# Attention with beacon keys, then a bilinear feed-forward net: the w1 and w2 products as seven block products, and a new order of all steps

## The chip, the cores and the metric

The kernel runs on one core of a Trainium2 chip. The metric is the device time of one execution in microseconds (us). A core has a matrix engine (PE; PEld is its weight load), VectorE (DVE), ScalarE (ACT), GpSimd (POOL) and SyncE (SP); the last two issue the transfers here. Matrix products go to PSUM, which holds 8 banks of 128 x 512 fp32 values; everything else is kept in SBUF.

## The reference, cut to what matters

```python
# q, k, v: (8, 8, 576, 64) fp32; beacon_k, beacon_v: (8, 8, 16, 64)
k_all = concatenate([beacon_k, k], axis=2)        # 592 keys
v_all = concatenate([beacon_v, v], axis=2)
scores = (1 / sqrt(64)) * matmul(q, k_all.T)      # beacons seen by all, k causal
a = exp(scores - max); a /= a.sum(-1) + 1e-9
x = matmul(a, v_all)                              # -> (4608, 512), heads side by side
y = ((x @ w1) * (x @ w2)) @ w3 @ w_out            # w1, w2: 512 x 1024; w3: 1024 x 1024; w_out: 1024 x 512
```

## The kernel before

Everything is in fp16 on the way into PE and in fp32 in PSUM. w3 @ w_out is computed once in the kernel (Wt, 1024 x 512), so that each token needs the products with w1, w2 and Wt only. The 4608 tokens are taken in two ways: attention goes by batch (8 batches of 576 tokens), the feed-forward part by chunks of 512 tokens (9 chunks, mc).

The order of all instructions is written out in one string, ORDER, a list of about 1170 short steps; the last line of the kernel walks through it and calls the function of each step. Each engine executes its own instructions in that order, and waits where a step needs what another engine has not finished. A step's last numbers are mostly PSUM banks, A or D name ACT or DVE, and S or P the queue that issues a transfer (SP or POOL). The steps are:

- loads: lq, lk, lv, lkb, lvb (q, k, v and beacons of a batch; batch 0's q and k come in fp32 on SP's queue, all others on POOL's, where they are cast to fp16), l1, l2 (quarters of w1, w2), l3 (128 rows of w3), lo (a quarter of w_out).
- q and k with the head's 64 values on the partitions: cast, tq/tk and eq/ek (transposes on PE and copies out of PSUM) or Dq/Dk (transposes by DMA, on SP's queue); tn and en for batch 0's beacons, tn waits for lkb 0.
- attention, in 13 groups g of score blocks per batch, four pairs of heads t: s (scores on PE, into two banks), exp (ACT, into the ring of 8 tiles), m (DVE, causal mask), v (PE, with the values), n (DVE: the reciprocal of the sums, then the scaling, into x16).
- x with its 512 columns on the partitions: x and ex (PE and a copy) or TX (by DMA), into xT.
- Wt: t3 and e3 (w3 transposed), f (PE, products with w_out), ew (copy).
- feed-forward, for 128 of the 1024 columns at a time (kf, 8 of them): a and b (PE, four matmuls each of 128x512), ea (the first product goes to SBUF in fp32, on ACT or DVE), eb (DVE: times the second product, into gT), then o (PE, 8 matmuls of 128x512 with Wt), eo (copy, on ACT or DVE) and st (out).

The lines of most use below: 546 (a, b on PE), 567 (o), 459 (f), 451 (t3), 474 (s), 505 (v), 531 (x), 484 (exp), 293 and 295 (ea and eo, on ACT and on DVE), 561 (eb), 494 (m), 516 and 517 (n), 377 (cast), 370 (l3). The trace writes w for w1 and w2 in SBUF, wo for w_out, va for v, and one or pair for PSUM banks. w3's rows lie in half of xT until they are used, so L370 writes xT.

```python
w316 = xT[:, :, ds(M // 2, 2 * DF)].rearrange("p a (c r) -> p a c r", c=2)
...
for line in ORDER.split(";"):
    kind, *args = line.split()
    ops[kind](*(int(arg) if arg.isdigit() else arg for arg in args))
```

Of the kernel before, what the change touches and what calls it, by code (L numbers as in the profile page):

```python
# [8 lines left out]
FP32 = mybir.dt.float32  # L9
# [59 lines left out]
f 3 0 7; f 2 0 6; exp 0 2 4; m 0 0 0; s 0 3 0; lv 0 4; f 3 1 7; exp 0 3 0; f 0 0 5; f 0 1 5; l3 7;
t3 1 4; exp 0 1 2; m 0 1 0; f 2 1 6; e3 1 D 4; s 0 4 0; s 0 5 2; lv 0 3; m 0 0 1; exp 0 4 0;  # L70
f 3 2 7; f 1 0 4; f 0 2 5; exp 0 5 2; lv 0 0; f 1 1 4; f 1 2 4; m 0 1 1; t3 5 3; lvb 0; f 3 3 7;
f 1 3 4; ew 3 A 7; tk 0 2 2; ew 1 D 4; l3 6; f 0 3 5; ek 0 2 A 2; f 2 2 6; ew 0 D 5; e3 5 A 3;
f 2 3 6; s 0 6 0; s 0 7 4; l2 2; ew 2 D 6; exp 0 6 0; f 5 0 7; l1 3; f 5 1 7; f 5 2 7; exp 0 7 4;
m 0 2 0; l3 4; f 5 3 7; ew 5 A 7; t3 7 6; lk 1 4 P; e3 7 A 6; lq 1 1 P; lkb 1; v 0 2 0 5;
v 0 1 0 7; lq 1 3 P; n 0 2 0 5; v 0 0 1 6; n 0 1 0 7; v 0 0 0 5; lk 1 0 P; s 0 8 2; s 0 9 0;
n 0 0 1 6; exp 0 8 2; t3 6 7; n 0 0 0 5; l2 3; v 0 1 1 6; e3 6 D 7; exp 0 9 0; f 7 0 5; m 0 2 1;
s 0 10 2; s 0 11 0; lq 1 2 P; m 0 3 0; exp 0 10 2; f 6 0 7; n 0 1 1 6; f 7 1 5; l2 1; t3 4 4;
exp 0 11 0; s 0 12 2; e3 4 D 4; l1 2; v 0 2 1 6; exp 0 12 2; m 0 3 1; tk 1 4 4; l1 1; f 7 2 5;
ek 1 4 D 4; f 7 3 5; n 0 2 1 6; lk 1 1 P; f 6 1 7; ew 7 A 5; v 0 3 0 4; lvb 1; tk 1 0 6; n 0 3 0 4;
tq 1 1 5; lq 1 4 P; ek 1 0 A 6; v 0 3 1 3; eq 1 1 D 5; x 0 0 4; lq 1 0 P; tq 1 3 6; n 0 3 1 3;  # L80
ex 0 0 A 4; f 6 2 7; f 6 3 7; eq 1 3 A 6; lk 2 0 P; tq 1 2 5; ew 6 D 7; x 0 3 4; eq 1 2 A 5;
x 0 1 6; x 0 2 3; ex 0 3 D 4; x 0 4 7; ex 0 1 A 6; lk 1 2 P; f 4 0 5; ex 0 2 D 3; f 4 1 5;
ex 0 4 A 7; f 4 2 5; f 4 3 5; lk 1 3 P; a 0 1 6; ew 4 A 5; a 0 7 7; ea 0 1 A 6; lv 1 0; a 0 0 6;
ea 0 7 A 7; lk 2 2 P; tq 1 4 7; tk 1 1 5; ea 0 0 A 6; lq 2 2 P; eq 1 4 D 7; a 0 4 4; ek 1 1 D 5;
lq 2 1 P; tq 1 0 6; b 0 7 7; eq 1 0 A 6; lv 1 3; tk 1 2 6; eb 0 7 7; b 0 1 5; ek 1 2 A 6; lv 1 4;
tk 1 3 6; lv 1 2; eb 0 1 5; a 0 3 7; ek 1 3 A 6; lv 1 1; ea 0 4 D 4; s 1 0 0; s 1 1 2; s 1 2 4;
# [101 lines left out]
def kernel(  # L188
# [93 lines left out]
    def bank(n):  # L282
        return shape(n, "one")
# [378 lines left out]
```

## Time and profile before

| | |
|---|---|
| median of 3 runs | 302.18 us (301.17 to 303.72) |
| the profiled execution, first to last instruction | 302.5 us |
| PE busy | 285.2 us (94%), 2850 matmuls |
| DVE, ACT, POOL busy | 149.9, 164.0, 131.8 us |
| mean granted TensorE clock | 0.966 |
| read from HBM, written to it | 39.32 MB, 9.44 MB |

How to read it: the profiled execution's 302.5 us stands 0.3 us above the median of the timed runs, so sums against it can be held against the median as they are. Busy is the time in which an engine had at least one instruction under way, so groups of pipelined matmuls overlap a little at their ends. The clock is in shares of 2.4 GHz: 1.00 is 2.4 GHz, 0.50 is 1.2 GHz.

### The profile page before, as it was taken

How to read it: one execution, taken by the hardware profiler on the slowest of the kernel's cores; microseconds unless marked ns; L12 is line 12 of the kernel's file. 1: busy time of each engine (PE TensorE's matmuls, PEld its weight loads, DVE VectorE, ACT ScalarE, POOL GpSimd, SP SyncE). 2: the span in 40 equal slices, each digit the busy share in tenths (PEclk: the TensorE clock that was granted, in tenths of full speed). 3: DMA queues.
4: the chain of work that ended last, by engine and by line, in shares of the span. 5: the costliest groups of instructions: out<-in, count | busy, mean ns of one | idle time of the engine just before them, and what ended most of it. 6: DMA issues, size and time to landing. Idle time of an engine off the chain costs nothing.

```text
span 302.5 us, 6941 instructions
## 1 busy us (share of the span) xinstructions
PE 285.2 (94%) x2850; PEld 153.2 (51%) x2850; DVE 149.9 (50%) x334; ACT 164.0 (54%) x214; POOL 131.8 (44%) x182
## 2 busy tenths in 40 slices
PE   6269999999999999997999999999999999999994
PEld 2154566456556465553545645554555455444441
DVE  4242574477278656671726535665462684134400
ACT  2246776687485578553628653755365265334332
POOL 8176888884297386760764375251002002000000
PEclk9657999999999999997999999999999999999999
DMA  7999999999999999999999999799316003500033
GB/s 186 242 205 183 184 185 153 129 158 135 173 197 141 144 187 173 155 144 153 147 151 152 131 183 197 96 167 205 50 49 145 0 2 113 106 0 0 2 139 138
DMA packets 159262, 40.85 MB, mean 135 GB/s; under 512 B 148736, under 2 KB 155392, under 8 KB 159232
## 3 DMA queue, kind: packets, MB, share of 16 engines
q0 software_dynamic: 114144, 25.83, 94.7%
q1 hardware_dynamic: 45088, 14.59, 32.3%
q8 instruction: 22, 0.36, 0.5%
q14 instruction: 8, 0.07, 0.1%
HBM read 39.32 MB, written 9.44 MB: 161 GB/s over the span
## 4 chain that ended last, share of the span: by engine, by line
PE 90%; DMA 4%; ACT 1%; DVE 1%; issue 1%; POOL 1%; POOLq 0%; DVEq 0%; ACTq 0%
PE one L546 42%; PE one L567 21%; PE one L505 10%; PE pair L474 9%; PE one L459 5%; DMA xT<-in_moe_w_dram 4%; PE one L451 1%; PE one L531 1%; PE one L395 1%; PE one L389 1%; DVE x L517 0%; ACT ring L484 0%; ACT gT L289 0%; POOL va L323 0%; DVE ring L494 0%
## 5 line engine op out<-in xcount | busy, mean ns | idle before, releaser
L546 PE MATMUL one<-xT,w 128*128 128x512 f16 x576 | 133.3, 381 | 2.5 <-issue 2.5
L484 ACT ACTIVATE ring<-pair 128x1024 f16<-128x1024 f32 x104 | 99.1, 1029 | 12.9 <-PE pair L474 12.7
L546 PEld LDWEIGHTS <-w 128*128 128x128 f16 x576 | 53.7, 98 | 63.8 <-issue 6.6
L561 DVE TENSOR_TENSOR gT<-one,asb 128x512 f16<-128x512 f32 x72 | 49.1, 689 | 46.4 <-ACT asb L293 25.2
L293 ACT ACTIVATE asb<-one 128x512 f32<-128x512 f32 x55 | 32.9, 597 | 65.7 <-PE one L546 50.9
L567 PE MATMUL one<-Wt,gT 128*128 128x512 f16 x288 | 66.1, 379 | 0.0
L580 POOL DMA_DIRECT2D out_dram<-st x28 | 15.8, 566 | 86.2 <-DVE rd L516 39.3
L567 PEld LDWEIGHTS <-gT 128*128 128x128 f16 x288 | 26.8, 98 | 30.0 <-issue 0.6
L323 POOL DMA_DIRECT2D va<-in_v_dram x40 | 34.0, 868 | 15.6 <-PE pair L474 8.6
L505 PEld LDWEIGHTS <-ring 128*128 128x128 f16 x960 | 34.4, 97 | 9.9 <-issue 2.4
L505 PE MATMUL one<-va,ring 128*128 128x65 f16 x960 | 37.5, 193 | 0.5 <-ACT gT L289 0.4
L293 ACT ACTIVATE st<-one 128x512 f32<-128x512 f32 x26 | 15.5, 597 | 35.5 <-PE one L567 35.5
L323 POOL DMA_DIRECT2D k<-in_k_dram x35 | 30.2, 863 | 7.8 <-DMA va<-in_v_dram 3.3
L517 DVE TENSOR_TENSOR x<-one,rd 128x384 f16<-128x384 f32 (+1 forms) x64 | 31.4, 491 | 2.2
L474 PE MATMUL pair<-qT,kT 64*128 64x80 f16 (+4 forms) x736 | 31.5, 231 | 0.7 <-ACT qT L289 0.7
L315 POOL DMA_DIRECT2D q<-in_q_dram x35 | 30.4, 872 | 2.9 <-DMA va<-in_v_dram 1.8
L474 PEld LDWEIGHTS <-kT 64*128 64x128 f16 x736 | 20.7, 98 | 17.5 <-issue 15.1
L516 DVE RECIPROCAL rd<-one 128x6 f32<-128x6 f32 (+1 forms) x64 | 11.8, 184 | 29.9 <-PE one L505 25.8
L494 DVE TENSOR_TENSOR ring<-ring,MD 128x768 f16<-128x768 f16 x32 | 17.7, 552 | 11.5 <-ACT ring L484 11.4
L459 PE MATMUL one<-wo,gT 128*128 128x512 f16 x64 | 17.3, 406 | 0.0
L494 DVE TENSOR_TENSOR ring<-ring,MX 128x384 f16<-128x384 f16 x32 | 11.3, 353 | 10.8 <-ACT ring L484 10.5
L295 DVE TENSOR_SCALAR asb<-one 128x512 f32<-128x512 f32 x17 | 11.6, 688 | 3.1 <-PE one L546 3.0
(53 smaller groups left out, 113.0 us busy)
## 6 DMA issues: line engine op xcount, KB each, us to landing
out_dram<-st POOLq DMA_DIRECT2D x28, 256.0 KB, 4.4
q<-in_q_dram POOLq DMA_DIRECT2D x28, 128.0 KB, 6.5
va<-in_v_dram POOLq DMA_DIRECT2D x24, 128.0 KB, 7.7
k<-in_k_dram POOLq DMA_DIRECT2D x21, 128.0 KB, 6.5
xT<-in_moe_w_dram POOLq DMA_DIRECT2D x8, 256.0 KB, 8.6
w<-in_moe_w_dram POOLq DMA_DIRECT2D x8, 256.0 KB, 7.2
out_dram<-st SPq DMA_DIRECT2D x8, 256.0 KB, 2.0
st<-in_k_dram SPq DMA_DIRECT2D x4, 288.0 KB, 5.4
```

Source lines behind the costliest of these rows:

```text
L293: nc.scalar.activation(dst, src, AF.Copy, scale=by)
L315: nc.gpsimd.dma_start(dst[:rows, c], src[b, :, ds(c * P, rows), :].rearrange("h s d -> s h d"))
L323: nc.gpsimd.dma_start(dst[ds(p0, rows), c], src[b, :, ds(s0, rows), :].rearrange("h s d -> s h d"))
L459: nc.tensor.matmul(bank(n), wT(r)[:, rt, :], wo16[:, rt, :], start=(rt == 0), stop=(rt == NFT - 1),)
L474: nc.tensor.matmul(shape(n, "pair")[:, hh, ds(col, w)], kT[ds(hh * 64, 64), t, ts(jt, P)], qT[ds(hh * 64, 64), t, ds(q0, w)],)
L484: nc.scalar.activation(held(b, g)[:, :, 0:GW], shape(n, "pair"), AF.Exp, scale=scale)
L494: nc.vector.tensor_tensor(blk, blk, msk, ALU.mult)
L505: nc.tensor.matmul(pv[:, 2 * at + hh, 0 : D + 1], held(b, g)[:, hh, ds(col, P)], va[:, jt, 2 * t + hh, 0 : D + 1], start=(jt == 0), stop=( ...
L517: nc.vector.tensor_tensor(x16s[b % NB2][:, ds(2 * h, ni), ts(t, P)].rearrange("p i (h d) -> p i h d", h=2), pv[:, 0 : 2 * ni, 0:D].rearran ...
L546: nc.tensor.matmul(bank(n), w12[:, kt, ds(i * DF + kf * P, P)], xT[:, kt, ds(mc * 512, 512)], start=(kt == 0), stop=(kt == NKT - 1),)
L561: nc.vector.tensor_tensor(gTs[mc % 2][:, kf, :], bank(n), asb[slot["asb", (mc, kf)]], ALU.mult)
L567: nc.tensor.matmul(bank(n), gTs[mc % 2][:, kf, ts(mt, P)], Wt[:, kf, :], start=(kf == 0), stop=(kf == NFT - 1),)
```

## The change

The feed-forward part goes by batch now, with halves of 288 tokens. For batches 1 to 7 the two products with w1 and w2 are seen as one product of 2 x 2 blocks: the token halves against the two halves of the 512 inner columns (a11, a12, a21, a22 in xT), and those against w1 and w2 (b11, b21, b12, b22). Four outputs are needed, namely both halves of the tokens with w1 and with w2. Instead of eight block products seven are made (step p, two matmuls of 128x288 each), from four sums S of blocks of x (step S, DVE, per batch) and four sums of blocks of w1, w2 (step T, DVE, once; one overwrites the first half of w2). PSUM adds up what it can: the order of one kf is

- p 5 and p 1 into two banks; ce (ACT) copies P5 to SBUF (es); c1 (ACT) copies P1 over P5 in its bank;
- p 6 adds to that bank (U2), p 2 adds to P1's bank (the first output);
- u (DVE): us = U2 + P5; then p 7 adds to U2's bank; p 3 goes into a third bank, t1 (DVE): us = P3 + us (the second output);
- t2 (DVE): es = U2 + P7 + P5 (the fourth output); then p 4 adds to U2's bank (the third output);
- g1 and g2 (DVE): the two elementwise products, 128x288, into gT.

Batch 0 is done plainly, in halves (a, b with four matmuls of 128x288, ea, and g). The factor 256 that ea applied is given by the ones column of v instead (ONE = 1/16, so that x is 16 times as large). gT holds two batches; o (now in four steps of two matmuls) still takes 128 tokens at a time.

The order is another one altogether. SP's queue has batch 0's k and q by pairs of heads; POOL's begins with batch 0's beacons and v. Here are POOL's first transfers before; in_moe_w is w1, w2 or w3 (L370 is l3, w3), in_v is lv, wo is w_out.

```order
L370 DMA xT<-in_moe_w_dram 128x1024
L323 DMA va_66<-in_v_dram 128x8x64
L370 DMA xT<-in_moe_w_dram 128x1024 x2
L348 DMA b_96<-in_beacon_k_dram 16x8x64
L373 DMA wo_61<-in_moe_w_out_dram 128x2x512 x2
...
L370 DMA xT<-in_moe_w_dram 128x1024
L373 DMA wo_61<-in_moe_w_out_dram 128x2x512
```

And the same queue from its start now (L412 is lkb, L387 lv, L425 a quarter of w1 or w2, L379 lq of batch 1).

```order
L412 DMA b_103<-in_beacon_k_dram 16x8x64
L387 DMA va_70<-in_v_dram 128x8x64
...
L387 DMA va_70<-in_v_dram 112x8x64
L425 DMA w_62<-in_moe_w_dram 128x4x256
L387 DMA va_70<-in_v_dram 80x8x64
L387 DMA va_70<-in_v_dram 128x8x64 x2
L420 DMA va_70<-in_beacon_v_dram 16x8x64
L379 DMA q_1_67<-in_q_dram 64x8x64
L425 DMA w_62<-in_moe_w_dram 128x4x256
```

The loads of w3 and w_out, their transposes and products (t3, f) moved behind batch 0's attention and feed-forward products. On PE, the first steps before were the transposes of batch 0's k and q and of w3 in turn (o16k and xT), then scores.

```order
L389 MATMUL one_104<-ident,o16k_90 128x96 [waits Pool_49]
L451 MATMUL one_104<-ident,xT 128x128 [waits Activation_49]
L389 MATMUL one_182<-ident,o16q_88 128x96
L389 MATMUL one_105<-ident,o16k_90 128x96 [waits Activation_49]
L451 MATMUL one_104<-ident,xT 128x128 [waits Activation_49]
L389 MATMUL one_105<-ident,o16q_89 128x96 [waits Activation_49]
```

PE's first steps now: the beacons' transposes, k and q of the first pair of heads (held in gT at that time), scores.

```order
L489 LDWEIGHTS b_103 [waits DMASW0_49]
L489 MATMUL ps<-ident,b_103 128x16 [waits Pool_49]
L453 LDWEIGHTS gT [waits DVE_49]
L453 MATMUL ps<-ident,gT 128x96
L453 MATMUL ps<-ident,gT 128x96 [waits Activation_49]
L537 LDWEIGHTS kT_74 [waits Activation_49]
L537 MATMUL ps<-qT_72,kT_74 128x128 [waits DVE_49]
```

The scores follow the first pair's transposes directly, with no w3 between. The third place is DVE in the middle of the feed-forward part. Before, one product in eb's form (L561) per kf stands among the steps of the next attention:

```order
L516 RECIPROCAL rd<-one_104 128x4
L517 TENSOR_TENSOR x_0_73<-one_104,rd 128x2x128
L516 RECIPROCAL rd<-one_2484 128x6
L517 TENSOR_TENSOR x_0_73<-one_2484,rd 128x3x128
L561 TENSOR_TENSOR gT_76<-one_2483,asb_78 128x512
L561 TENSOR_TENSOR gT_76<-one_104,asb_79 128x512
L561 TENSOR_TENSOR gT_76<-one_105,asb_77 128x512
L494 TENSOR_TENSOR ring<-ring,MX 128x2x192
```

Now u, t1, t2, g1, g2 (L686, L689, L692, L695, L700) of two or three kf at a time stand in turn (batch 5):

```order
L686 TENSOR_TENSOR us_84<-ps,es_80 128x288
L579 RECIPROCAL rd<-ps 128x6
L580 TENSOR_TENSOR x_0_77<-ps,rd 128x3x128
L689 TENSOR_TENSOR us_84<-ps,us_84 128x288
L692 TENSOR_TENSOR es_80<-ps,es_80 128x288
L695 TENSOR_TENSOR gT<-ps,us_84 128x288
L686 TENSOR_TENSOR us_85<-ps,es_81 128x288
L700 TENSOR_TENSOR gT<-ps,es_80 128x288
```

For each kf there are now five instructions of 128x288 per batch, each of which waits for PE or for an earlier one of the five, where there was one eb of 128x512 per chunk (and an ea, on DVE in 17 of 72 cases). Step counts that changed, in the whole list, before (now): a and b 72 + 72 with 512 columns (16 + 16 with 288), p 0 (392), ea 72 (16), eb or g 72 (16 + 112), ce, c1, u, t1, t2 0 (56 each), S 0 (28), T 0 (16), tq and tk 9 + 9 (14 + 14), Dq and Dk 30 + 30 (25 + 25), x 15 (20), TX 25 (20). Scores, exp, m, v, n, t3, f and o have the same instructions as before.

```diff
 ORDER = """
-consts 0; lk 0 0 S; lk 0 3 S; l3 0; consts 1; spin 10 7; lq 0 1 S; lv 0 2; lk 0 1 S; lq 0 3 S;
...
+lk 0 0 S; consts 0; lq 0 0 S; lkb 0; lk 0 1 S; lv 0 1; consts 3; spin 8 7; lq 0 1 S; lk 0 2 S;
...
-    xT = const.tile([P, NKT, M], FP16, name="xT")
+    xTs = [const.tile([P, NKT, S], FP16, name=f"xT_{i}") for i in range(NB2)]
+    Ss = [const.tile([P, 4, 2, HT], FP16, name=f"S_{i}") for i in range(NB2)]
+    T124 = const.tile([P, 3, 2, DF], FP16, name="T124")
...
-    gTs = [const.tile([P, NFT, 512], FP16, name=f"gT_{i}") for i in range(2)]
-    asb = [const.tile([P, 512], FP32, name=f"asb_{i}") for i in range(NASB)]
+    gT = const.tile([P, NFT, NG2], FP16, name="gT")
+    es = [const.tile([P, HT], FP32, name=f"es_{i}") for i in range(NES)]
+    us = [const.tile([P, HT], FP32, name=f"us_{i}") for i in range(NUS)]
...
-    w316 = xT[:, :, ds(M // 2, 2 * DF)].rearrange("p a (c r) -> p a c r", c=2)
+    def w316(r):
+        return sts[r].bitcast(FP16)[:, 0:DF]
...
+    def S_(b, i):
+        sv = Ss[b % NB2]
+        (a11, a12), (a21, a22) = quad(b)
+        in0, in1, op = {
+            1: (a21, a22, ALU.add),
+            2: (sv[:, 0], a11, ALU.subtract),
+            3: (a11, a21, ALU.subtract),
+            4: (a12, sv[:, 1], ALU.subtract),
+        }[i]
+        nc.vector.tensor_tensor(sv[:, i - 1], in0, in1, op)
...
+    def p(b, kf, i, n):
+        (a11, a12), (a21, a22) = quad(b)
...
+        mov, sta = {
+            1: (a11, b11),
+            2: (a12, b21),
+            3: (sv[:, 3], b22),
+            4: (a22, t4),
+            5: (sv[:, 0], t1),
+            6: (sv[:, 1], t2),
+            7: (sv[:, 2], t3),
+        }[i]
+        for j in (0, 1):
+            nc.tensor.matmul(
+                half(n),
+                sta[:, j],
+                mov[:, j],
+                start=(j == 0 and i in (1, 3, 5)),
+                stop=(j == 1),
+                skip_group_check=True,
+            )
...
-    def ea(mc, kf, e, n):
-        scaled(e, asb[take("asb", (mc, kf), NASB)], bank(n), GS)
+    def ea(b, kf, h, e, n, i):
+        copy(e, es[i], half(n))
...
+    def ce(n, i):
+        nc.scalar.copy(es[i], half(n))
+
+    def c1(na, ne):
+        nc.scalar.copy(half(ne), half(na))
+
+    def u(n, i, j):
+        nc.vector.tensor_tensor(us[j], half(n), es[i], ALU.add)
+
+    def t1(n, j):
+        nc.vector.tensor_tensor(us[j], half(n), us[j], ALU.add)
+
+    def t2(n, i):
+        nc.vector.tensor_tensor(es[i], half(n), es[i], ALU.add)
+
+    def g1(b, kf, n, j, us=us):
+        nc.vector.tensor_tensor(
+            gT[:, kf, ds((2 * b) % 4 * HT, HT)], half(n), us[j], ALU.mult
+        )
```

## Rows read from the trace of the kernel before

**Rows 1.** The page: the span in 40 slices of 7.56 us, three of its lines.

```profile
PE   6269999999999999997999999999999999999994
PEclk9657999999999999997999999999999999999999
GB/s 186 242 205 183 184 185 153 129 158 135 173 197 141 144 187 173 155 144 153 147 151 152 131 183 197 96 167 205 50 49 145 0 2 113 106 0 0 2 139 138
```

**Rows 2.** Chain of work that ended last, first 52 us: start, duration, what.

```profile
3.28 12.01 DMA xT<-in_moe_w_dram
...
20.59 0.65 ACT qT L289
21.28 1.46 PE pair L474 x22
...
48.23 0.86 PE one L531 x16
...
50.82 1.29 PE one L546 x6
```

**Rows 3.** The same chain, its longest pieces over the whole span.

```profile
257.03 27.74 PE one L546 x128
284.77 13.83 PE one L567 x64
```

**Rows 4.** The same chain, its last piece.

```profile
298.62 0.60 ACT st L293
```

**Rows 5.** Stretches: length, then PE, PEld, DVE, ACT, POOL busy, clock, DMA share, GB/s.

```profile
10.00:15.00 5.00, 0.66 (x6) 0.45 (x6) 1.31 (x3) 0.64 (x1) 0.26 (x1) 0.50 1.24 238
15.00:20.00 5.00, 3.27 (x34) 2.85 (x35) 2.02 (x4) 1.65 (x3) 3.75 (x6) 0.50 1.21 203
...
25.00:30.00 5.00, 5.00 (x38) 2.32 (x35) 1.51 (x3) 3.58 (x4) 2.81 (x6) 0.87 1.92 176
```

**Rows 6.** DVE and POOL in order of time, start of the kernel.

```profile
4.27 0.66 DVE L377 CAST o16k<-st 96x768 f16<-96x768 f32 x1 [1.96 <-DMA st<-in_k_dram]
8.44 0.56 DVE L377 CAST o16q<-st 96x768 f16<-96x768 f32 x1 [1.58 <-DMA st<-in_q_dram]
...
2.34 0.95 POOL L323 DMA_DIRECT2D va<-in_v_dram  x1
14.74 0.57 POOL L370 DMA_DIRECT2D xT<-in_moe_w_dram  x1 [5.60 <-DMA va<-in_v_dram]
```

**Rows 7.** Groups by line and shape: count, busy us, mean ns of one, idle before.

```profile
L517 DVE TENSOR_TENSOR x<-one,rd 128x384 f16<-128x384 f32 x32 | 17.8, 558 | 1.1
L517 DVE TENSOR_TENSOR x<-one,rd 128x256 f16<-128x256 f32 x32 | 13.6, 425 | 1.1
L494 DVE TENSOR_TENSOR ring<-ring,MD 128x768 f16<-128x768 f16 x32 | 17.7, 552 | 11.5 <-ACT ring L484 11.4
L494 DVE TENSOR_TENSOR ring<-ring,MX 128x384 f16<-128x384 f16 x32 | 11.3, 353 | 10.8 <-ACT ring L484 10.5
L289 ACT COPY xT<-one 128x320 f16<-128x320 f16 x2 | 0.9, 432 | 0.0
L293 ACT ACTIVATE asb<-one 128x512 f32<-128x512 f32 x55 | 32.9, 597 | 65.7 <-PE one L546 50.9 <-DVE gT L561 11.8 <-DVE x L517 2.4
```

**Rows 8.** The page's costliest groups, the scores and the products with v.

```profile
L505 PE MATMUL one<-va,ring 128*128 128x65 f16 x960 | 37.5, 193 | 0.5 <-ACT gT L289 0.4
L474 PE MATMUL pair<-qT,kT 64*128 64x80 f16 (+4 forms) x736 | 31.5, 231 | 0.7 <-ACT qT L289 0.7
```

**Rows 9.** DVE and ACT in order of time, 175 to 200 us.

```profile
184.41 1.28 DVE L561 TENSOR_TENSOR gT<-one,asb 128x512 f16<-128x512 f32 x2
199.39 0.18 DVE L516 RECIPROCAL rd<-one 128x4 f32<-128x4 f32 x1 [2.00 <-PE one L505]
199.61 0.42 DVE L517 TENSOR_TENSOR x<-one,rd 128x256 f16<-128x256 f32 x1
189.26 2.86 ACT L484 ACTIVATE ring<-pair 128x1024 f16<-128x1024 f32 x3 [0.58 <-PE pair L474]
```

More of the change, by code (lines that the diff above doesn't have):

```diff
@@ L69 @@
[L69 to L74, printed above, removed]
@@ L248, with pair, half @@
     psum = ctx.enter_context(tc.tile_pool(name="psum", bufs=1, space=PSUM))
-    tiles = {
-        0: psum.tile([P, 2, 512], FP32, name="pair"),
-        6: psum.tile([P, 512], FP32, name="one_6"),
-        7: psum.tile([P, 512], FP32, name="one_7"),
-    }
-    shared = {2: ctx.enter_context(ExitStack()), 4: ctx.enter_context(ExitStack())}
-    form = {}
-    ctx.enter_context(tc.manual_schedule())
-    def shape(n, what):
-        if n in (2, 3, 4, 5) and form.get(n // 2) != what:
-            at = 2 * (n // 2)
-            shared[at].close()
-            pool = shared[at].enter_context(
-                tc.tile_pool(
-                    name=f"{what}_{at}",
-                    bufs=1,
-                    space=PSUM,
-                    side="left" if at == 2 else "right",
-                    reuse_waits="tile",
-                )
-            )
-            form[n // 2] = what
-            if what == "pair":
-                tiles[at] = pool.tile([P, 2, 512], FP32, name="pair")
-            else:
-                for i in (at, at + 1):
-                    tiles[i] = pool.tile([P, 512], FP32, name=f"one_{i}")
-        return tiles[n]
+    ps = psum.tile([P, 8, 512], FP32, name="ps")
+    ctx.enter_context(tc.manual_schedule())
     def bank(n):
-        return shape(n, "one")
+        return ps[:, n]
     def bank16(n):
         return bank(n).bitcast(FP16)
+    def pair(n):
+        return ps[:, ds(n, 2)]
+    def half(n):
+        return ps[:, n, 0:HT]
     def copy(engine, dst, src):
@@ L483, in exp @@
     def exp(b, g, n):
-        nc.scalar.activation(held(b, g)[:, :, 0:GW], shape(n, "pair"), AF.Exp, scale=scale)
+        nc.scalar.activation(held(b, g)[:, :, 0:GW], pair(n), AF.Exp, scale=scale)
     def m(b, t, h):
@@ new lines, in S_, with T_ @@
+    def S_(b, i):
[8 more added lines that the diff above has]
+        nc.vector.tensor_tensor(sv[:, i - 1], in0, in1, op)
+    def T_(c, i):
+        cols = ds(c * 256, 256)
+        b11, b21 = w12[:, 0:2, cols], w12[:, 2:4, cols]
+        b12, b22 = (w12[:, ds(j, 2), ds(DF + c * 256, 256)] for j in (0, 2))
+        t1, t2, t4 = (T124[:, j, :, cols] for j in range(3))
+        out_, in0, in1 = {
+            1: (t1, b12, b11),
+            2: (t2, b22, t1),
+            3: (b12, b22, b12),
+            4: (t4, b21, t2),
+        }[i]
+        nc.vector.tensor_tensor(out_, in0, in1, ALU.subtract)
@@ L573, in o, with eo, st @@
             )
-    def eo(mc, mt, e, n):
-        scaled(e, sts[take("st", (mc, mt), NST)][:, 0:DM], bank(n), float(1.0 / GS))
-    def st(mc, mt, e):
+    def eo(i, e, n, j):
+        scaled(e, sts[j][:, 0:DM], bank(n), float(1.0 / GS))
+    def st(i, e, j):
         queue = nc.gpsimd if e == "P" else nc.sync
-        queue.dma_start(out[ds(mc * 512 + mt * P, P), :], st_of((mc, mt))[:, 0:DM])
+        queue.dma_start(out[ts(i, P), :], sts[j][:, 0:DM])
     def spin(reps, n):
```

412 lines of the change are left out of this document (256 added, 156 removed).

## The prediction

> **What bounds the kernel now.** I read the page's slices first, then the chain of work that ended last, then single groups. The slices show PE at nine tenths or more from the sixth slice to the end, and the holes before that [rows 1]: PE has little to do until 20 us and runs at 0.50 of its clock there [rows 5]. The chain says why. It holds a 12 us wait for w3's rows (xT<-in_moe_w), PE's transposes of w3 stand in that wait, and the first scores come only at 21.28 us [rows 2]. From then on the chain is PE's own work almost without a gap: the first w1 product starts at 50.82 us [rows 2], the last stretch is 128 matmuls of products in 27.74 us and 64 of o in 13.83 us [rows 3], that is 216.7 and 216.1 ns for 512 columns, one directly behind the other. The last copy begins at 298.62 [rows 4] and the span ends at 302.5, 0.3 us above the median of the runs, so the tail is 3.9 us. DVE and ACT are about half busy, so their steps are hidden. Two things can therefore make the kernel faster: fewer columns on PE, and less idle time ahead of the first product. And DVE must stay hidden.
>
> **PE's work behind the first product.** The stretch from the first product to the end is 302.5 - 50.8 = 251.7 us now. What the change does to it:
>
> - Products with w1 and w2. Before 576 matmuls of 512 columns, x 0.2167 = 124.8 us. Now 784 (p) and 128 (a, b) of 288 columns. None of that width is in the trace. 128 columns take 0.86 / 16 = 54 ns [rows 2]; a straight line from there to 216.7 ns gives 122 ns, and 288/512 of 216.7 gives 121.9. Both ends are so near that I take 122: 912 x 0.122 = 111.3 us, a gain of 13.5. A floor per instruction could spoil this, but products with v of 65 columns, each with its own weight load, take 37.5 us / 960 = 39 ns [rows 8], so 122 ns has no floor near it. I allow 125, which is 2.7 us more.
> - The w3, w_out product stood ahead of the first w1 product and now stands behind it: 64 x 0.2167 = 13.9 for f and 64 x 0.054 = 3.5 for t3, together 17.4 us, moved and not added.
> - More transposes on PE instead of by DMA: behind the first product 12 for q, k and 15 for x in place of 5 and 10, with four matmuls each: (28 + 20) x 0.054 = 2.6 us. Their copies go to DVE and ACT. SP's queue gets 15 fewer.
> - Scores, exp, v, o: the same instructions.
>
> Sum: 251.7 - 13.5 + 17.4 + 2.6 = 258.2 us.
>
> **The start.** Now SP has only batch 0's k and q, by pairs of heads. Before, the first k tile was being cast at 4.27 us [rows 6]; the next 288 KB follow at about 1.2 us each (186 to 242 GB/s in the first slices [rows 1]), so the first pair is there at some 5.5 us. Cast, transposes and copy took from 17.64 to 21.28 us in the old chain, of which its last copy is 0.65 [rows 2], with a wait for w3's transposes inside; without it I count 2 us, so the first scores come at 7.5 (up to 10 if the beacons land late: PE's transposes of them stand ahead). Then ACT is the longest: 13 exps at (2.86 - 1.03) / 2 = 0.92 us spacing [rows 9] and 8 copies, shorter than the 0.65 us of the old ones of 576 columns [rows 2], some 0.53 each, make 16.2 us, to 23.7. v must be in too. While k and q were being loaded, a v load issued at 2.34 us landed at 14.7 [rows 6], so I expect the last of v's five at about 17, in time for the second half of the groups. Behind the last exp stand the last v, n and x with a few us, and PE's clock will be at 0.50 for part of this, as it was between 10 and 20 us [rows 5]. I take 29 us for the first product, in place of 50.8. Bounds: 25.5 if nothing waits; 35 by the loads, since the list asks 6.4 MB up to there and the first four slices moved (186 + 242 + 205 + 183) x 7.56 us = 6.2 MB in 30.2 us [rows 1].
>
> So 29 + 258.2 = 287.2 us if DVE, ACT and the loads stay hidden.
>
> **DVE and ACT.** ACT loses 55 ea of 597 ns [rows 7] and gets 112 copies (ce, c1) of 288 columns. 432 ns for 320 columns [rows 7] bounds each from above; a line to 597 gives 0.41. That adds some 46 us and takes 33, on an engine at 54%: hidden, except that p 6 waits for c1 each time.
>
> DVE gets 280 steps of 128x288 in place of 72 eb, 28 S and 16 T. The trace has 256 and 384 columns from PSUM: 425 and 558 ns [rows 7], so 288 last 425 + 32 x 1.04 = 458 ns. But two in a row take 1.28 us where one takes 0.69 [rows 9]: the second begins some 0.09 before the first ends. In a queue a step of 288 thus costs 0.37. S and T work on fp16 in SBUF, as the masks do: 353 and 552 ns for 384 and 768 [rows 7], so 452 for 576, 0.37 in a queue. From the first S to the end the list holds, for DVE: 280 x 0.37 = 104, S 28 x 0.37 = 10, n 48 x 0.62 = 30 (the reciprocal's 0.18, 0.04 to the scaling's start [rows 9], and 0.34 or 0.47), m 47 x 0.37 = 17, copies 16 x 0.6 = 10, together 171 us. For PE: p 784 x 0.122 = 96, o 282 x 0.216 = 61, the scores 73 of 104 groups = 22, v 48 of 64 = 28, the rest 3, together 210 us. DVE is at 81% of PE's load, where before it was at half.
>
> Hidden on the whole is not hidden at each place. If the engines could run ahead of each other without end, the stretch would take 210 us. The eight PSUM banks hold two or three kf, some 5 us. I cut the list into pieces of about 5 us and took in each the larger sum of PE, DVE and ACT: 214. In pieces of 3 us it is 221. I take 4 us for this, with 0 and 11 as its ends. The forecast is 287.2 + 4 = **291 us**.
>
> A rule of the Trainium skill speaks against this change: VectorE: DVE Perf Modes, in the section on the TRN2 errata, says that a fixed cost is paid per instruction, so that tiles should have 512 elements or more, and gives (N + 151)/0.96 ns for an fp32 tensor_tensor, 457 ns at 288. The line through the rows of this trace gives the same length, 458. If the fixed part were paid in full each time, the time would be the first rival's, 301 us; by the row with two steps in 1.28 us it is the forecast's.
>
> **Rivals.**
>
> 1. DVE's fixed part isn't hidden by its queue, because each step waits for PE or for an earlier step of its own. Then the 467 DVE instructions of that stretch cost 0.09 more, 171 + 42 = 213 against PE's 210. The pieces of the list then add between 3 (by whole batches) and 21 us (at 5 us); with 14, the time is 287 + 14 = 301 us, no change. For it: in the present trace DVE mostly waits, and full queues are rare. Against: a DVE that is late has a queue, and then the row with two in 1.28 us applies.
> 2. On the slower side: DVE becomes the bound in the p steps. Steps that need the result just before them on DVE start 0.04 after its end (reciprocal to scaling, 199.39 + 0.18 to 199.61 [rows 9]), and u, t1, g1 form such a chain. If this held for all, a step cost 0.49, DVE's sum was 228, and the stretch followed it: 18 us above PE, and some 5 for uneven pieces, 287 + 23 = 310 us. It makes the kernel slower than 305 from about 0.48 us a step. Against: the list puts two or three kf in turn, so that mostly another kf's step lies between.
> 3. The loads bound the middle of the start. Up to batch 1's first p the list asks for 14.3 MB, which the slices had moved at 81 us [rows 1]; my sum has that place at 75. It costs 6 us: 297. For it: many of these are the small packets of q, k and v. Against: some of the bytes are for batches 3 and 4.
> 4. The block form does not shorten PE's time, because 288 columns cost as much as half of 512 and a bit: with 140 ns it gains nothing, 912 x 0.018 = 16 us more, 307. The 39 ns for 65 columns speak against it; it gets no more than 2%.
>
> **How the numbers follow.** The forecast 291 has 0.58 (its own range 284 to 297: the bounds of the start, 25.5 to 35, and of the uneven pieces, not all at one end). Rival 3 (297) 0.14, rival 1 (301) 0.14, rival 2 (310) 0.10, rival 4 0.02, and 0.02 for less than 284. The range 284 to 304 leaves out the slower rivals and a little below. About 1% is what a measurement of this kernel tells from no change, that is 299.2 to 305.2. Faster: 0.58, the most of rival 3 and the 0.02, a share of rival 1, 0.75. Within 1%: the most of rival 1 and a little of rivals 2 and 3, 0.14. Slower: 0.11.
>
> **What the profile would show.** Right: the first scores before 10 us, the first 288-column product near 29, runs of these at 122 ns, PE busy in all slices from the fifth on, and DVE at 75 to 80% of the span with steps of 458 ns. For rival 1 and 2: PE idle before p 4 and p 7, released by DVE, and DVE at 90% or more in the slices of batches 3 to 5. For rival 3: PE or ACT released by q<-in_q or xT and wo loads between 30 and 75 us. The prediction would be wrong above all if the three engines' hand-over per kf (ce, c1, u, t2) takes longer than the two or three kf in flight cover, since then each of 56 kf pays.

## The result, and the profile after

The changed kernel takes 294.07 us (median of 4 runs, 292.65 to 295.61) against 302.95 us before (301.17 to 305.5): a ratio of 0.9728, with a 95% interval of 0.9673 to 0.9782. It is 2.7% faster. The forecast was 291 us, with a range of 284 to 304. The profiled execution has a span of 293.9 us. Medians and ranges below leave out single executions that lie more than 1.5% above the fastest of the same kernel, one in run 6 and two in the first of run 8.

The page's slices come first, as in [rows 1]; a slice is now 7.35 us, and DVE's line is added.

```profile
PE   6778999999999999999999999799999999999994
...
DVE  4958567672677889898779889797899888899940
...
PEclk9559999999999999999999999999999999999999
...
GB/s 190 217 175 172 196 183 183 178 142 143 110 168 181 146 165 122 178 176 149 140 133 181 117 157 188 159 46 120 175 172 3 43 120 38 36 3 71 39 71 143
```

PE is full from the fifth slice on, with one notch in the 26th, whose cause is shown below. DVE stands at 8 or 9 in most slices of the second half. The start of the chain of work that ended last (start, duration, what) answers to [rows 2]:

```profile
8.20 9.54 DMA va<-in_beacon_v_dram
17.74 0.14 issue
17.88 1.15 PE ps L568 x18
...
30.68 3.11 PE ps L662 x24
33.79 0.14 PE ps L459 x4
33.93 5.39 PE ps L662 x44
```

The start waits for v: its last piece (the beacons' part) is issued at 8.2 and lands at 17.7, and at once the first v product runs. The first scores came at 8.0 (21.28 before). The first 288-column product (L662 is a and b, on batch 0) begins at 30.68 in place of 50.82, and 44 of them take 5.39 us, that is 122.5 ns each. The end of the same chain answers to [rows 3] and [rows 4] (L651 is p, L706 is o):

```profile
272.67 5.02 PE ps L651 x40
...
283.96 6.06 PE ps L706 x28
290.02 0.02 issue
290.04 0.60 ACT st L360
```

Products of o cost 216 ns as before, and the tail behind the last copy's start is 3.9 us again. The three stretches of [rows 5], with the same columns (length, PE, PEld, DVE, ACT, POOL busy, clock, DMA share, GB/s):

```profile
10.00:15.00 5.00, 3.52 (x41) 2.28 (x40) 4.57 (x10) 3.74 (x6) 1.34 (x2) 0.50 1.67 204
15.00:20.00 5.00, 3.53 (x55) 2.71 (x53) 2.33 (x5) 3.40 (x5) 4.85 (x7) 0.50 2.10 168
25.00:30.00 5.00, 3.71 (x84) 3.40 (x84) 4.75 (x14) 4.34 (x8) 4.35 (x7) 1.00 1.88 178
```

PE has work there now, though not all the time. The groups by line and shape (count, busy us, mean ns of one, idle before), the new kinds beside those of [rows 7]:

```profile
L700 DVE TENSOR_TENSOR gT<-ps,es 128x288 f16<-128x288 f32 x64 | 28.8, 450 | 6.1 <-PE ps L651 3.7 <-ACT es L356 1.4 <-PE ps L662 0.6
L686 DVE TENSOR_TENSOR us<-ps,es 128x288 f32<-128x288 f32 x56 | 25.2, 451 | 9.4 <-PE ps L651 5.8 <-ACT ps L683 2.7 <-ACT ring L547 0.4
...
L680 ACT COPY es<-ps 128x288 f32<-128x288 f32 x56 | 22.1, 404 | 25.1 <-PE ps L651 23.2 <-DVE S L620 1.1
L683 ACT COPY ps<-ps 128x288 f32<-128x288 f32 x56 | 21.7, 393 | 3.6 <-PE ps L651 1.6
```

A DVE step of 288 columns lasts 450 ns (458 was worked out from [rows 7]), ACT's copies 393 to 404 (410 worked out). DVE and ACT still wait for PE here. The other way round, PE's one long wait is the notch: 1.5 us at 186.7, for an output copy of ACT, which had waited for the store out of the tile that it was to fill.

```profile
186.03 0.60 ACT L360 ACTIVATE st<-ps 128x512 f32<-128x512 f32 x1 [4.58 <-DMA out_dram<-st]
```

In order of time, two DVE steps one behind the other, as in [rows 9]:

```profile
257.46 0.46 DVE L692 TENSOR_TENSOR es<-ps,es 128x288 f32<-128x288 f32 x1
257.83 0.45 DVE L695 TENSOR_TENSOR gT<-ps,us 128x288 f16<-128x288 f32 x1
```

The second starts 0.37 us after the first, before the first has ended. Of the 245 pairs of such steps that stand directly one behind the other, 178 start 0.36 to 0.385 us apart.

For what the steps cost PE I added up, from the records of all its matmuls behind the first product, by how much two starts lie further apart than the columns of the first one take, where that is over 30 ns. Below this is called PE's gaps. It is 11.7 us before and 15.5 us after, and 13.6 in a second execution of the changed kernel (after_again below). Most of it lies where PE goes from scores (tiles of 64*128) to any other product or back:

```profile
131.65 0.41 PE L651 MATMUL ps<-S,T 128*128 128x288 f16 x2
131.89 0.41 PE L651 MATMUL ps<-xT,w 128*128 128x288 f16 x2
132.23 0.39 PE L537 MATMUL ps<-qT,kT 64*128 64x128 f16 x4
132.56 0.60 PE L706 MATMUL ps<-Wt,gT 128*128 128x512 f16 x2
```

From the first pair to the second it takes 0.24 us, and from the second pair, with the same columns, to the scores 0.34. Each such switch costs 0.097 us on the median, before as after. Behind the first product there were 64 of them, 6.5 us, and now there are 122, 11.8 us, since the new order puts the scores into smaller pieces. What is left of the gaps is 5.2 us before (2.7 of it in one stall at 138.3), 3.7 after (1.7 of it the notch) and 1.8 in the second execution, which has no notch.

### The profile page after: what moved, and what is told of

The parts are those of the page before. It is cut to its first block, busy times and chain, and to the rows that moved or that the text cites. A ratio compares the mean times of both kernels' runs of the same rounds, so it can differ in the third digit from the quotient of the medians.

```text
span 293.9 us, 8221 instructions
## 1 busy us (share of the span) xinstructions
PE 280.4 (95%) x3244; PEld 187.2 (64%) x3244; DVE 227.5 (77%) x600; ACT 180.8 (62%) x287; POOL 133.2 (45%) x185
## 4 chain that ended last, share of the span: by engine, by line
PE 67%; DMA 20%; issue 3%; POOL 3%; ACT 2%; DVE 2%; SPq 1%; POOLq 0%; DVEq 0%; ACTq 0%
PE ps L651 26%; PE ps L706 15%; PE ps L568 7%; DMA out_dram<-st 7%; PE ps L537 6%; PE ps L662 5%; PE ps L522 5%; DMA k<-in_k_dram 4%; DMA va<-in_beacon_v_dram 3%; DMA xT<-x 3%; DMA va<-in_v_dram 3%; POOL va L387 2%; PE ps L594 2%; ACT ring L547 1%; PE ps L515 1%
## 5 line engine op out<-in xcount | busy, mean ns | idle before, releaser
L547 ACT ACTIVATE ring<-ps 128x1024 f16<-128x1024 f32 x104 | 101.1, 1028 | 23.4 <-PE ps L537 21.0
L706 PE MATMUL ps<-Wt,gT 128*128 128x512 f16 x288 | 77.9, 380 | 0.0
L719 POOL DMA_DIRECT2D out_dram<-st x31 | 17.4, 563 | 99.7 <-ACT st L360 47.1
L651 PEld LDWEIGHTS <-w 128*128 128x128 f16 x448 | 42.2, 98 | 17.9 <-issue 3.1
L651 PE MATMUL ps<-xT,w 128*128 128x288 f16 x224 | 44.0, 286 | 1.5 <-ACT st L360 1.5
L651 PE MATMUL ps<-S,T 128*128 128x288 f16 x224 | 44.9, 286 | 0.1
L651 PE MATMUL ps<-S,w 128*128 128x288 f16 x224 | 43.3, 286 | 0.0
L568 PE MATMUL ps<-va,ring 128*128 128x65 f16 x960 | 39.6, 196 | 2.3 <-DMA va<-in_beacon_v_dram 1.5
L651 PEld LDWEIGHTS <-T 128*128 128x128 f16 x336 | 31.0, 97 | 15.4 <-issue 2.0
L387 POOL DMA_DIRECT2D va<-in_v_dram x40 | 34.1, 864 | 13.0 <-PE ps L568 10.8
L537 PE MATMUL ps<-qT,kT 64*128 64x80 f16 (+4 forms) x736 | 37.1, 231 | 2.0 <-DVE qT L356 1.7
L379 POOL DMA_DIRECT2D q<-in_q_dram x35 | 29.8, 854 | 15.6 <-DMA qT<-q 7.5
L706 PEld LDWEIGHTS <-gT 128*128 128x128 f16 x288 | 25.5, 98 | 17.7 <-issue 2.8
L387 POOL DMA_DIRECT2D k<-in_k_dram x35 | 29.8, 860 | 11.1 <-PE ps L459 2.2
L700 DVE TENSOR_TENSOR gT<-ps,es 128x288 f16<-128x288 f32 x64 | 28.8, 450 | 6.1 <-PE ps L651 3.7
L580 DVE TENSOR_TENSOR x<-ps,rd 128x384 f16<-128x384 f32 (+1 forms) x64 | 31.4, 491 | 2.2
L537 PEld LDWEIGHTS <-kT 64*128 64x128 f16 x736 | 20.0, 97 | 20.1 <-issue 16.5
L686 DVE TENSOR_TENSOR us<-ps,es 128x288 f32<-128x288 f32 x56 | 25.2, 451 | 9.4 <-PE ps L651 5.8
L360 ACT ACTIVATE st<-ps 128x512 f32<-128x512 f32 x23 | 13.7, 597 | 29.5 <-PE ps L706 24.7
L689 DVE TENSOR_TENSOR us<-ps,us 128x288 f32<-128x288 f32 x56 | 25.1, 450 | 2.1 <-PE ps L651 0.5
```

The source lines that it names most:

```text
L379: nc.gpsimd.dma_start(dst[:rows, c], src[b, :, ds(c * P, rows), :].rearrange("h s d -> s h d"))
L387: nc.gpsimd.dma_start(dst[ds(p0, rows), c], src[b, :, ds(s0, rows), :].rearrange("h s d -> s h d"))
L537: nc.tensor.matmul(pair(n)[:, hh, ds(col, w)], kT[ds(hh * 64, 64), t, ts(jt, P)], qT[ds(hh * 64, 64), t, ds(q0, w)],)
L547: nc.scalar.activation(held(b, g)[:, :, 0:GW], pair(n), AF.Exp, scale=scale)
L568: nc.tensor.matmul(pv[:, 2 * at + hh, 0 : D + 1], held(b, g)[:, hh, ds(col, P)], va[:, jt, 2 * t + hh, 0 : D + 1], start=(jt == 0), stop=( ...
L580: nc.vector.tensor_tensor(x16s[b % NB2][:, ds(2 * h, ni), ts(t, P)].rearrange("p i (h d) -> p i h d", h=2), pv[:, 0 : 2 * ni, 0:D].rearran ...
```

## Experiments

Each lot ran on one chip with the kernel before beside it, whose median lay between 301.7 and 303.0 us in the four lots. The changed kernel was run once more with the second lot:

> The changed kernel as it is, timed in the same rounds as the three others: 294 us within 1.

It took 294.02 us (292.92 to 294.25), ratio 0.9727 (0.969 to 0.9764).

**1. The block form taken out, the order kept.** The seven block products become the eight plain ones, in the same places of the order. The steps S, T, ce, c1 and t2 go, and ACT copies two of the outputs in the places of u and t1; the main part of the edit:

```diff
-            3: (sv[:, 3], b22),
-            4: (a22, t4),
-            5: (sv[:, 0], t1),
-            6: (sv[:, 1], t2),
-            7: (sv[:, 2], t3),
+            3: [(a11, b12), (a12, b22)],
+            5: [(a21, b12)],
+            6: [(a22, b22)],
+            7: [(a21, b11)],
+            4: [(a22, b21)],
```

> The changed kernel's order and tiles, but batches 1 to 7 make all eight block products (p 3 makes two), no S and T, and the outputs are copied by ScalarE in the places of u and t1. PE gets 56 x 2 matmuls of 288 columns more, 13.7 us at 122 ns, and VectorE loses three of five steps per kf. Theory 1 (PE bounds the kernel behind the first product, VectorE is hidden, the seven products bring their whole 13 us): 294 + 13.7 less at most 4 us of waits that go away, 303 to 308 us. Theory 2 (VectorE's steps cost most of what the seventh product saves, and the gain came from the new start): 296 to 300 us.

Measured 308.49 us (307.71 to 309.2), ratio 1.0207 (1.0152 to 1.0263). The eighth product costs 308.5 - 294.0 = 14.4 us, where its columns say 13.7. So the block form pays in full what its columns say, and DVE (153.3 us of work here, 227.5 in the changed kernel) takes nothing of it back. The new order alone is 2% slower than before: it begins its products at 29.9, some 21 us earlier, has to do the product of w3 with w_out (17.4 us) and more transposes (2.3) behind that, and has the same 122 switches to and from the scores, 5.3 us more than before. So the gain comes with the block form, and the new order by itself gave none. The block form in the old order was not run.

**2. DVE's slack, from below.** The two sums u and t1 are left out.

```diff
-        nc.vector.tensor_tensor(us[j], half(n), es[i], ALU.add)
+        return
...
-        nc.vector.tensor_tensor(us[j], half(n), us[j], ALU.add)
+        return
```

> The changed kernel without u and t1, so that two of the five outputs' sums are left out (g1 multiplies by ones). VectorE does 112 steps fewer, 41 us at 0.37, and p 7 and g1 no longer wait for them. Theory 1: only the waits at uneven places go, 0 to 4 us, 290 to 294 us. Theory 2 (VectorE sets the time of the p stretches): 280 to 286 us.

Measured 292.82 us (292.57 to 294.38), ratio 0.970 (0.9645 to 0.9755). DVE has 189.9 us of work, 37.6 less, and the kernel gains 1.2 us, which the intervals do not tell from nothing: DVE is hidden. Of PE's gaps the switches stay as they are, 11.8 us, and the rest falls to 0.9.

**3. DVE's slack, from above.** One extra step for each group of seven products, and then two.

```diff
+        if b:
+            nc.vector.tensor_tensor(scratch, half(n), es[i], ALU.mult)
```

> The changed kernel with one VectorE step more per kf in batches 1 to 7 (g2 once more into a scratch tile, 128x288), 56 steps, 20.7 us at 0.37. Theory 1 (VectorE at 81% of PE's load with queue prices, hidden except in dense stretches): 3 to 10 us slower than 294, that is 297 to 304. Theory 2 (VectorE already sets the time of the p stretches): all of it, 313 to 317 us.

> Two extra VectorE steps of 128 x 288 for each group of seven block products, where the run with one step came out at 304.8 and the changed kernel at 294; VectorE then has 268 us of work. Theory: VectorE's slack is used up by the first extra step, half of which was paid, so that the second is paid in full, 56 times 0.365 us = 20.4: 322 to 327. Rival: what the first step cost was a delay at hand-overs and not a lack of throughput, and the second is again half hidden: 312 to 317.

One step: 304.83 us (303.51 to 305.7), ratio 1.0083 (1.0053 to 1.0113), 10.8 more than the changed kernel. Two: 330.43 us (329.93 to 330.75), ratio 1.094 (1.0895 to 1.0985), another 25.6. The second step costs more than either theory had: 25.6 / 56 = 0.457 us for each, and not the 0.37 of a queue. The trace shows that this second step is held (L701 is g2, L705 and L706 the extra steps):

```profile
244.87 0.45 DVE L701 TENSOR_TENSOR gT<-ps,es 128x288 f16<-128x288 f32 x1
245.24 0.44 DVE L705 TENSOR_TENSOR scratch<-ps,es 128x288 f16<-128x288 f32 x1
245.71 0.46 DVE L706 TENSOR_TENSOR scratch<-ps,es 128x288 f16<-128x288 f32 x1
```

In all 56 places the first extra step starts 0.36 to 0.375 us behind g2, and the second 0.48 us behind the first. All three read the same bank and the same es; only the second writes the tile that the step ahead of it writes. So its price is that of a step that waits for the one before, and no run here shows what a second step with a tile of its own would cost. Two stretches of the run with two steps, in the columns used above:

```profile
100.00:120.00 20.00, 17.86 (x194) 11.08 (x192) 17.70 (x48) 9.86 (x20) 10.47 (x14) 1.00 1.96 143
240.00:260.00 20.00, 16.60 (x161) 9.87 (x159) 19.30 (x50) 7.98 (x15) 0.54 (x1) 1.00 0.07 14
```

PE, 20.00 of 20 us in both stretches of the changed kernel, is down to 17.86 and 16.60, and DVE is at 17.7 to 19.3. Over the span DVE is at 82% with two extra steps, 81% with one and 77% with none. The first extra step added 245.8 - 227.5 = 18.3 us of DVE's work and 10.8 us of time, so that an estimate of the room left on DVE is 7.5 us. An extra step also holds its PSUM bank until it is done; the runs do not part this from DVE's time.

**4. Weights ahead of v in the start.** Three rows of w3 and half of w_out (1.3 MB in fp16) are loaded right behind batch 0's beacons; the rows get a tile of their own.

```diff
-lk 0 0 S; consts 0; lq 0 0 S; lkb 0; lk 0 1 S; lv 0 1; consts 3; spin 8 7; lq 0 1 S; lk 0 2 S;
+lk 0 0 S; consts 0; lq 0 0 S; lkb 0; l3 0; l3 2; l3 3; lo 0; lo 1; lk 0 1 S; lv 0 1; consts 3; spin 8 7; lq 0 1 S; lk 0 2 S;
```

> The changed kernel with three rows of w3 and two quarters of w_out (1.3 MB) loaded directly behind batch 0's beacons on the POOL queue, ahead of its v, as the kernel before did; the steps that use them stay where they are, and the three rows have a tile of their own. Theory 1 (the first product waits for v on the POOL queue): v lands and the first product starts 5 to 8 us later, and the end comes 4 to 7 us later, 298 to 301 us. Rival (the order of loads does not matter to the start, only their sum): within 1.5 us of 294.

Measured 300.27 us (299.53 to 302.74), ratio 0.9944 (0.9906 to 0.9982), 6.2 more. The chain of that run, with the times of v and of the first product:

```profile
3.65 11.40 DMA wo<-in_moe_w_out_dram
15.05 0.28 issue
15.33 8.07 DMA va<-in_beacon_v_dram
23.40 0.04 issue
23.44 1.15 PE ps L569 x18
...
36.43 3.11 PE ps L663 x24
```

v lands 5.7 us later, at 23.4, and the first product comes 5.75 us later, at 36.43. The start is v's, and what stands ahead of v on POOL's queue is paid for at the end.

**5. v ahead of the weights.** Only the order of two loads is changed: lvb 0 moves up behind lkb 0, l1 0 down behind v's last piece.

```diff
-lk 0 0 S; consts 0; lq 0 0 S; lkb 0; lk 0 1 S; lv 0 1; consts 3; spin 8 7; lq 0 1 S; lk 0 2 S;
+lk 0 0 S; consts 0; lq 0 0 S; lkb 0; lvb 0; lk 0 1 S; lv 0 1; consts 3; spin 8 7; lq 0 1 S; lk 0 2 S;
```

> The changed kernel with two loads of batch 0 in another order on GpSimd's queue: beacon v right behind beacon k, and the first w1 quarter behind the last piece of v, so that all of v is asked for before any weight. Theory: the first v product waits for the last piece of v that lands (17.7 us in the changed kernel, its issue at 8.2), and the first 288-column product follows it; v then lands 1 to 2 us earlier and the end moves by as much: 292 to 293.5 us, the first v product at 16 to 17, the first product at 29 to 30. Rival: the start is bound elsewhere by then (the quarters of w1 and w2, which come later in the queue, or the q, k pieces): the first product stays at 30.7 or comes later, and the time stays at 294 within 0.5 us.

Measured 291.98 us (291.41 to 293.98), ratio 0.968 (0.9641 to 0.9718), 2.0 us below the changed kernel of the same lot. The first v product begins at 16.5 (17.6 there), the first product at 28.86 (30.95 there), both as expected. What holds the start now is seen in the chain:

```profile
9.77 10.09 DMA w<-in_moe_w_dram
19.86 0.02 issue
19.88 0.43 DVE T L633
...
28.86 3.11 PE ps L662 x24
```

DVE's first difference of weights (T) waits for w1's quarter until 19.86, and the division by the row sums stands behind it in DVE's order.

**6. That wait taken away too.** The six T steps of the first two quarters move behind batch 0's products of the quarter, from T 0 1 near 20 us to just ahead of T 0 3 and T 1 3, which overwrite their input.

```diff
-v 0 1 1 3; exp 0 8 0; T 0 1; v 0 2 0 4; lk 1 0 P; eq 1 4 D 5; tq 1 0 2; T 0 2; s 0 10 6;
+v 0 1 1 3; exp 0 8 0; v 0 2 0 4; lk 1 0 P; eq 1 4 D 5; tq 1 0 2; s 0 10 6;
```

> The run with all of v asked for ahead of the weights, and the six VectorE differences of the first two quarters of w1 and w2 moved behind batch 0's products of that quarter, to just ahead of the step that overwrites their input. In that run the chain had w1's first quarter land at 19.86 us, and VectorE's first difference behind it, ahead of the division by the row sums that the attention output waits for. Theory: VectorE no longer waits there for a weight, and the first 288-column product begins 0.5 to 1.5 us earlier (28.9 there): 290.5 to 291.5 us. Rival: ScalarE's exponentials, of which three stand behind that step in the chain, set the start: first product at 28.9 and 292 us as there; or the differences come too late for the first block product, which then waits: over 292.

Measured 291.43 us (291.28 to 294.8), ratio 0.9673 (0.9625 to 0.9722). The first product comes at 28.4, 0.5 us earlier, but the time is that of run 5 within what these runs tell. The chain goes another way now:

```profile
21.38 6.65 DMA k<-in_k_dram
28.03 0.05 issue
28.08 0.40 PE ps L444 x4
28.47 1.55 PE ps L647 x12
```

k of batch 1 lands at 28.03, and its transposes (L444) stand ahead of the first products on PE. The last copies of x, at the end of the way through the exponentials, end at 28.31 on DVE and 28.34 on ACT, just ahead of the first product too. So DVE's wait was worth 0.5 us, and behind it two things end nearly together, the next load on POOL's queue and the exponentials; the run does not part them.

**7. Output tiles in eight slots.**

```diff
-        scaled(e, sts[j][:, 0:DM], bank(n), float(1.0 / GS))
+        scaled(e, sts[i % 8][:, 0:DM], bank(n), float(1.0 / GS))
```

> The run before this in the list, and each output tile staged in slot (tile number mod 8) of the eight staging tiles, where the changed kernel writes slots 0 to 3 by its list. Three of the executions profiled show a wait of 1.7 to 3.6 us at 185 to 193 us in which ScalarE waits for a store out of the slot that it is to fill, and TensorE for ScalarE. Theory: it is gone, and what other waits on stores there are: 0 to 2 us less than the run before it, 289 to 291. Rival: the stores are slow because the queues are full there, and the wait moves to the next load: no difference, within 0.5 us.

Measured 292.64 us (291.3 to 293.19), ratio 0.9666 (0.9634 to 0.9698): no difference. The profiled execution of run 6 has no such wait either, so there was nothing to take away in it; in run 5 the wait was 2.14 us, behind a store that landed 11.5 us after its issue. The wait comes and goes between executions, and these runs don't settle what it is worth.

**8. The product of w3 and w_out left out.** Its place behind the first product was the largest cost in the forecast's sum, 17.4 us. Three runs:

```diff
-            nc.tensor.transpose(pt[:, rt, :], w316(r)[:, ts(rt, P)], ident)
...
-                wTs[i][:, rt, :],
-                wo16[:, rt, :],
...
-        copy(e, Wt[:, r, :], bank(n))
```

> The changed kernel without the product of w3 and w_out: its 64 transposes, 64 products of 512 columns and 16 copies are left out, and the tile that would hold the product is filled with ones once; the loads of w3 and w_out stay. The output is therefore not the reference's. Theory: in the new order this work lies behind the first product and TensorE is the bound there, so that it costs its full time, 17.4 us: 276 to 278. Rival: it fills time in which TensorE would wait anyway (for loads of batch 1 and 2 and for VectorE), and so costs less than half of that: 285 or more.

> As the run without the product of w3 and w_out, and the loads of w3 and w_out (12 issues of GpSimd) left out too; the tile that would hold the product is again filled with ones, so the output is not the reference's. That run began its first block product at 80.4 us, as the changed kernel does (79.8), and TensorE stood still for 12 of the 40 us ahead of it. Theory: TensorE stood waiting for transfers, which share GpSimd's queue with these 12 loads; without them the q and k of batch 1 and 2 and w1, w2 land earlier, the first block product begins at 62 to 68 us, and the time is 275 to 283. Rival: it stood waiting for the order of the steps (buffers that come free and hand-overs between the engines), which is unchanged: the first block product stays at 78 to 81 and the time at 293 to 299.

> The first run without the product of w3 and w_out again, with one fault of it mended: there VectorE filled the whole tile with ones in one step of 3.47 us at 39.7, and TensorE waited 3.4 us for what stood behind it. Here each of the eight rows is filled by itself, on VectorE, where its copy from PSUM stood; transposes, products and the other copies stay left out, the loads stay in, the output is not the reference's. Theory, after the run without the loads: in this order the left-out work filled time in which TensorE waits for ScalarE's exponentials of batch 1 and for q and k of batch 2, so that only a small part of its 17.4 us comes back: first block product at 76 to 79 us against 79.8, time 290 to 294. Rival: the fault cost more than the wait behind it (by the order of the queues, and the clock that fell to 0.71 to 0.87 in the two stretches that follow), and most of the 17.4 us comes back: first block product under 72, time under 286.

The first gave 296.3 us (295.5 and 297.0; ratio 0.981, 0.9748 to 0.9871), the second, without the loads too, 296.65 us (293.36 to 297.7; ratio 0.9789, 0.9736 to 0.9842). In both, DVE filled the whole tile in one step of 3.47 us, and PE waited 3.4 us behind it. In the third the tile is filled row by row, and that wait is gone: 294.83 us (293.38 to 296.75), ratio 0.972 (0.9688 to 0.9753). That is the time of the changed kernel with 17.4 us of PE's work less. The stretches of the third run, and then those of the changed kernel:

```profile
40.00:60.00 20.00, 15.29 (x255) 11.82 (x253) 15.70 (x43) 14.18 (x19) 14.99 (x21) 1.00 1.79 182
60.00:80.00 20.00, 13.16 (x136) 8.05 (x137) 10.00 (x26) 8.96 (x14) 18.91 (x24) 0.66 2.45 151
```

```profile
40.00:60.00 20.00, 20.00 (x271) 13.72 (x269) 14.61 (x38) 14.54 (x19) 14.99 (x20) 1.00 1.79 182
60.00:80.00 20.00, 20.00 (x237) 12.43 (x236) 11.31 (x30) 14.78 (x20) 16.17 (x20) 1.00 2.51 127
```

Without the work PE stands still for 4.7 + 6.8 = 11.5 of these 40 us, its clock is granted at 0.66 on the mean in the second half (0.50, that is 1.2 GHz, from 65 to 70 us), and the first block product comes at 77.9 us in place of 79.6. So part of the time left out came back as matmuls at the lower clock; PE is busy for 8.7 us between 60 and 75, of which an estimate is that some 4 would go at the full clock. What PE and ACT wait for from 48 to 80 us in the third run (us in total, times, longest):

```profile
ACT kT L356 <- PE ps L459: 5.5, 1, 5.5
ACT ring L538 <- PE ps L528: 3.3, 6, 1.2
...
PE ps L459 <- DMA k<-in_k_dram: 2.7, 2, 1.4
PE ps L528 <- ACT ring L538: 2.5, 2, 1.6
...
PE ps L459 <- DMA q<-in_q_dram: 1.4, 1, 1.4
```

They are ACT's exponentials of batch 1 (L528 is s) and q and k of the next batches (L459 are their transposes). The work of w3 had filled that time. That the loads of w3 and w_out hold it is refuted by the second run, which began its first block product at 81.8, with the 3.4 us wait in it, although these 12 loads of POOL's queue were gone. What is left is the order of the steps, that is, which step is put ahead of which on PE, ACT and POOL (the loads of q and k with them), and the clock; this is argued from the waits and not shown. Whether another order would begin batch 1's exponentials earlier, and so gain from leaving the work out, wasn't tried.

## Why the prediction was right, step by step

- **Products by columns, -13.5 us: right.** 122.5 ns a matmul, forecast 122. By the starts of all their matmuls, PE spends 12.5 us less on them without the gaps; run 1 has 14.4 us for the eighth product. Rival 4 (a price of 140 ns) is out.
- **The start, 29 us: right in its mechanism, 1.7 us short.** First scores 8.0 (7.5), v in at 17.7 (17), first product 30.7 (29, bounds 25.5 and 35). v was named as what must be in, but the sum had ACT's 13 exponentials as the longest; runs 4 and 5 show that the first product follows v: 5.75 us later where v lands 5.7 later, and 2.1 earlier where the first v product comes 1.1 earlier. Three of the exponentials stand behind the first v products in that chain, so they were not free to run from the first scores on, as the sum had them.
- **The w3, w_out product, +17.4 us: the columns were right, their meaning was not.** The step counted them as a cost of the new order. Run 8 shows that in this order the same time passes without them: the first block product came at 77.9 us, with PE waiting for ACT and for the q and k loads, and with a lower clock. The sum came out because PE's work and that limit are nearly the same length there: the forecast had the first block product at 75, rival 3 had 81, the trace has 79.6, with PE busy all the way. That is luck of the sum. And half of rival 3 was there: a limit besides PE's work lay ahead of the first block product, at about 78 us in run 8, though it was not the loads of w3 and w_out.
- **Transposes on PE, +2.6 us: right.** By the starts of all their matmuls, PE spends 2.3 us more on them.
- **Scores, "the same instructions": put at nothing, and cost 5.3 us.** The instructions are the same, but they stand in smaller pieces between the other products, and PE pays 0.097 us for each of 58 more switches. They are there in run 1 and run 2 as well, so neither the block form nor DVE makes them.
- **Uneven pieces, +4 us (0 to 11): right in size only by luck.** The 4 us were meant for waits at hand-overs between PE, DVE and ACT. Outside the switches and the notch, PE's gaps are 1.8 to 2.0 us, and 0.9 in run 2, so that such waits are at most 2 us and DVE's part of them about 1.
- **The whole stretch.** From the first product to the end it is 293.9 - 30.7 = 263.2 us, and 261.3 in the second execution; the forecast had 258.2 + 4 = 262.2. It fits because the switches, which the sum did not have, stand where most of the 4 us were, and because the stall of 2.7 us of the profile before, which is in the 251.7 that the sum starts from, is gone.
- **DVE hidden, at 0.37 a step in a queue: right, with little to spare.** 178 of 245 pairs show that price. DVE is at 77% of the span, the forecast had 75 to 80. Rivals 1 and 2 did not come true at 280 steps, since taking 112 of them away gains only 1.2 us (run 2). They are close, all the same: 56 extra steps cost 10.8 us.

The rule that was weighed, VectorE: DVE Perf Modes, section on the TRN2 errata, in the Trainium skill, gave 457 ns at 288 columns as an estimate; the trace has 450 for one step. The same page of the Trainium skill, in its section "The DRAIN you can't avoid", says that a next op that is not held starts earlier. The rows at 257.46 and 257.83, 0.37 us apart, agree. Where a step did wait for the one before, as the second extra step of run 3, the start came 0.48 us later.

## What to carry to other kernels

A product taken away from the engine that sets the time pays its whole column time only as long as the engines that put the blocks together stay hidden; how far they are from showing is measured by adding dummy steps (here 112 steps less gained 1.2 us and 56 more cost 10.8). Each dummy needs a tile of its own to write, since here the one that wrote the tile of the step before it was held. A finer order has a price on the bounding engine itself: here 58 more switches between scores and other products cost 5.3 us, more than all waits for DVE and ACT. To see which part of a change pays, run its parts apart: the new order without the block form was slower than the kernel before. Work that is moved to where the bounding engine looks full is not necessarily a cost: leave it out once, and see whether the engine then stands still. In a start that is bound by one queue, put the bytes that the first long chain needs ahead of everything else: here 1.3 MB ahead of v cost 6 us, and v ahead of one quarter of the weights gained 2.

## What was not expected of the hardware

PE's granted clock in the start was not the same in two executions of the same kernel: 0.50 from 10 to 20 us in the first, shown above, and 1.00 in the second, of which this is one stretch.

```profile
15.00:20.00 5.00, 4.05 (x60) 3.22 (x61) 2.54 (x6) 3.83 (x5) 5.00 (x7) 1.00 2.03 167
```

The first product came at 30.7 and 30.9 all the same, because the start waits for v: a clock at half cost nothing there. Later in the span, with the work of w3 left out (run 8), the clock fell to 0.50 (1.2 GHz) from 65 to 70 us, behind stretches in which PE stood waiting (busy for 3.02 us from 55 to 60 and 1.83 from 60 to 65); in the changed kernel, with PE busy all the time there, it stayed at 1.00 (2.4 GHz).

The price of a switch between scores and other products, 0.097 us, was the same in the kernel before, in the changed kernel and in runs 1, 2 and 5 to 7: in each of them the middle nine tenths of the switches lie between 0.094 and 0.101 us.
